# Weight blocks of a two-layer mixing kernel: when they are loaded, and in which tiles

## The chip, the core and the metric

The kernel runs on one core of one Trainium2 chip. A core has five engines that each work through their own instructions in order and wait for each other by semaphores: TensorE (PE, matmuls), VectorE (DVE), ScalarE (ACT), GpSimd (POOL), and SyncE (SP), which here only issues DMAs. The metric is the time of one execution on the device in microseconds. All times are of one program on one core.

## The reference

Everything is float32 in the reference. Its third part, in which the change lies, is this (batch 8, 576 tokens, 512 channels, 256 hidden tokens, 1536 hidden channels):

```python
def _moe2_ref(x, w_tok1, w_tok2, w_ch1, w_ch2) -> np.ndarray:
    xt = x.transpose(0, 2, 1)
    h = np.maximum(xt @ w_tok1, 0.0) @ w_tok2
    u = x + h.transpose(0, 2, 1)
    h2 = np.maximum(u @ w_ch1, 0.0) @ w_ch2
    return (u + h2).astype(np.float32)
```

Before it stand an attention over pooled keys (`_attn_ref`) and a first mixing `_moe_ref`, that ends in `u + relu(u @ w_ch)`; its result is the `x` above. The inputs arrive as float64 words (the host does no arithmetic), so a weight has to be turned into float32 on the chip before it is used.

## The kernel before

**Numbers.** A float32 value is kept as a pair of values in a rounded format, a high part and a rest (`h`, `l`), and a product is three matmuls: high by high, high by rest, rest by high. The high part is made by an ACT cast, the rest by a subtraction on DVE or POOL.

**Stages.** Up to about 555 us run the attention and most of the first mixing. From 555 to 779.4 us runs the *token stretch*, batch by batch (8 of them, one about every 28 us): `emit_ch` (L863 on) ends the first mixing, eight groups of 12 matmuls into one PSUM bank each, that DVE drains into `u` (L878); `emit_tr` transposes `u` on PE (L173), and ACT and DVE copy the transposes out as a pair (L893, L894); `emit_tok1` makes the hidden tokens (drained by ACT L912 and DVE L913); `emit_tok2` makes the second token product (drained by DVE L928). Then `channel_mix` does the two channel products as one level of Strassen's scheme, seven products in place of eight. The first product (779.4 to 1064.9 us) has six chunks of columns with six passes each; a pass, `first_pair(c, i)`, is 7 products of 6 matmuls of 128x384, 42 matmuls. Of them `p1` (ACT L1264), `u2` (DVE L1268), `p5` (ACT L1277, DVE L1278 and L1281) and four outputs `g` are drained. The bank of `p1` is added to again by the third product (A12), the bank of the copy at L1277 by the sixth (S4), that of L1281 by the seventh (A22), so PE can't go on with these three before ACT or DVE has read them. The second product follows (to 1335.3 us).

**Weight blocks.** `weight_steps(m, wd, tags, gaps)` (L955) writes the weights of the two channel products, in the form in which the products use them, to the DRAM tensor `scr_w[m]`: m = 0 is `w_ch1` (6 blocks of width 256), prepared during the token stretch; m = 1 is `w_ch2` (12 blocks of width 128), prepared during the first product. A block goes through these steps:

- `load`: two DMAs of the raw words into `ws`. For m = 0 each is held back by a copy of one element on ACT (L976) from the `u` drained last (`gate`).
- `conv` for two halves: ACT takes Abs (L992), DVE four operations (L993, L994, L998, L1002) that put the bits of the float32 together in `wm`.
- `sums`: POOL L1011 and L1012, DVE L1013 and L1014, that form Strassen's sums in `wsum`.
- `split` for two halves, two pieces each: ACT casts into a piece `wo` (L1023), POOL or DVE subtracts (L1024), a DMA stores the piece to `scr_w` (L1025).

The steps stand in a list `wq`, with empty steps (`gaps`) between them. `wstep()` takes one: in the token stretch after every second group of `emit_ch` and twice in `emit_tok2` (six a batch, as many as a block has), in the first product after every product.

**Order.** The program is written as a list of operations; a scheduler turns it into one order for each engine, with the place in the program as priority, and sets waits where regions of tiles overlap. Each named place in SBUF (`kr`, `vr`, `R1`, `n0` ...) holds one tile at a time. `Units` (L1072) hands out operand containers: `HOME_E` 14 for even, `HOME_O` 11 for odd chunks (`R1` 3, `e` 3, `Z0` 5). An operand takes two, a chunk's seven take 14, so the next chunk's are prepared as far as containers are free. `HOME_R` are four buffers (`n0` to `n3`) for raw columns (`raw_n`) from which operands are split (ACT L1125, DVE L1126) and differences formed (DVE L1129). At the last chunk `more_raws` makes raw buffers of the odd containers that have come free. `free_s` (from `HOME_S`) is the list of buffers that `first_pair` drains into; its outputs `g` leave by a DMA (L1258).

Of the kernel before, what the change touches and what calls it, by code (L numbers as in the profile page):

```python
# [10 lines left out]
F32R = mybir.dt.float32r  # L11
U32 = mybir.dt.uint32
# [52 lines left out]
def tile_attn_moe(  # L65
# [56 lines left out]
    def st(tag, shape, dt, name=None):  # L122
        need(tag)
        return sb.tile(shape, dt, tag=tag, name=name or tag)
# [227 lines left out]
    bdk = st("bdk", [128, 4, 144], F32)  # L352
    vbh = st("vbh", [128, 4, 128], F32R)
    vlh = st("vlh", [128, 4, 2, 64], F32R)
# [588 lines left out]
    def rotate(tags):  # L943
        n = [0]

        def alloc(shape, dt, name):
            tag = tags[n[0] % len(tags)]
            n[0] += 1
            return st(tag, shape, dt, name)

        return alloc
# [3 lines left out]
    def weight_steps(m, wd, tags, gaps):  # L955

        NH_ = 256 // wd
        quads = [(g, j, h) for g in range(3) for h in range(NH_) for j in range(2)]  # L960
        ws_t, wm_t, wsum_t, wo_t = (rotate(x) for x in tags)
        whole = wd == 128
        raw = {}

        def load(i):
            g, j, h = quads[i]
            behind = gate[0]
            if whole:
                t = ws_t([128, 2, 2, wd, 2], U32, f"ws{m}_{i}")
                t = [t[:, kk] for kk in range(2)]  # L970
            else:
                t = [ws_t([128, 2, wd, 2], U32, f"ws{m}_{i}_{kk}") for kk in range(2)]
            if behind is not None:

                for x in t:
                    nc.scalar.copy(out=x[0:1, 0, 0:1, 0].bitcast(F32), in_=behind)  # L976
            for kk in range(2):
                if m == 0:
                    src, r, c0 = w_ch1, (2 * kk + j) * 128, g * 256 + h * wd
                else:  # L980
                    src, r, c0 = w_ch2, (6 * kk + 2 * g + j) * 128, h * wd
                src = src[r:r + 128, :].bitcast(U32).rearrange("p (h c t) -> p h c t", h=2, t=2)
                nc.sync.dma_start(out=t[kk], in_=src[:, :, c0:c0 + wd, :])
            raw[i] = [t, None, None]

        def conv(i, kk):
            if kk == 0:
                raw[i][1] = wm_t([128, 2, 2, wd], F32, f"wm{m}_{i}")
            t = raw[i][0][kk]
            x = raw[i][1][:, kk]  # L990
            xu = x.bitcast(U32)
            nc.scalar.activation(out=x, in_=t[:, :, :, 1].bitcast(F32), func=ACTF.Abs)  # L992
            nc.vector.tensor_scalar(out=x, in0=x, scalar1=F64_FLOOR, scalar2=None, op0=ALU.max)  # L993
            nc.vector.tensor_scalar(  # L994
                out=xu, in0=xu, scalar1=3, scalar2=0x3FFFFFFF,
                op0=ALU.logical_shift_left, op1=ALU.bitwise_and,
            )
            nc.vector.scalar_tensor_tensor(  # L998
                out=xu, in0=t[:, :, :, 1], scalar=0xC0000000, in1=xu,
                op0=ALU.bitwise_and, op1=ALU.bitwise_or,  # L1000
            )
            nc.vector.scalar_tensor_tensor(  # L1002
                out=xu, in0=t[:, :, :, 0], scalar=29, in1=xu,
                op0=ALU.logical_shift_right, op1=ALU.bitwise_or,
            )

        def sums(i):
            x = raw[i][1]
            s = raw[i][2] = wsum_t([128, 4, wd], F32, f"wsum{m}_{i}")
            a11, a21, a12, a22 = x[:, 0, 0], x[:, 0, 1], x[:, 1, 0], x[:, 1, 1]  # L1010
            nc.gpsimd.tensor_tensor(out=s[:, 0], in0=a21, in1=a22, op=ALU.add)  # L1011
            nc.gpsimd.tensor_tensor(out=s[:, 2], in0=a11, in1=a21, op=ALU.subtract)  # L1012
            nc.vector.tensor_sub(out=s[:, 1], in0=s[:, 0], in1=a11)  # L1013
            nc.vector.tensor_sub(out=s[:, 3], in0=a12, in1=s[:, 1])  # L1014

        def split(i, half):
            x, s = raw[i][1:3]
            parts = ((x[:, 1], 2, A12, nc.gpsimd), (x[:, 0, 0:1], 1, A11, nc.gpsimd)) if half == 0 else (
                (s[:, 0:2], 2, S1, nc.vector), (s[:, 2:4], 2, S3, nc.vector))
            g, j, h = quads[i]  # L1020
            for n, (src, k, o0, eng) in enumerate(parts):
                o = wo_t([128, 2, 2, wd], F32R, f"wo{m}_{i}_{half}{n}")[:, 0:k]
                nc.scalar.copy(out=o[:, :, 0], in_=src)  # L1023
                eng.tensor_sub(out=o[:, :, 1], in0=src, in1=o[:, :, 0].bitcast(F32))  # L1024
                nc.sync.dma_start(out=scr_w[m][:, g, o0:o0 + k, j, h * 2 * wd:(h + 1) * 2 * wd],  # L1025
                                  in_=o.bitcast(F32).rearrange("p k a c -> p k (a c)"))

        def nothing():
            pass

        steps = []
        for i in range(len(quads)):
            ahead = []
            if i == 0:
                steps += [lambda: load(0)] + [nothing] * gaps[0]
            if i + 1 < len(quads):
                ahead = [lambda i=i: load(i + 1)] + [nothing] * gaps[0]
            for f, n in ((lambda i=i: conv(i, 0), gaps[1]), (lambda i=i: conv(i, 1), gaps[2])):
                steps += [f] + [nothing] * n
            if m == 1:  # L1040
                steps += ahead
            for f, n in ((lambda i=i: sums(i), gaps[3]), (lambda i=i: split(i, 0), gaps[4]),
                         (lambda i=i: split(i, 1), gaps[5])):
                steps += [f] + [nothing] * n
            if m == 0:
                steps += ahead
        return steps

    wq = []
    gate = [None]  # L1050

    def wstep(n=1):
        while wq and n > 0:
            wq.pop(0)()
            n -= 1
# [2 lines left out]

    HOME_W = [f"w{i}" for i in range(13)] + ["zt1", "q0", "q1", "pt0", "pt1", "zt0", "tmp0", "tmp1"]
    HOME_E = (("Z1", 5), ("Xh", 3), ("Xl", 3), ("R0", 3))  # L1060
    HOME_O = (("R1", 3), ("e", 3), ("Z0", 5))
    HOME_R = (("n0", 1), ("n1", 1), ("n2", 1), ("n3", 1))
    HOME_S = ["vbh", "vlh", "vbl", "vll", "bdk", "vlr", "t1", "stg1"]

    def channel_mix():
        class Units:
# [31 lines left out]
        even = Units(HOME_E, F32R, "ope")  # L1098
        odd = Units(HOME_O, F32R, "opo")
        raws = Units(HOME_R, F32, "raw")  # L1100
        free_w = list(HOME_W)
        free_s = list(HOME_S)

# [76 lines left out]
        def pump(n):  # L1180
            while queue and n > 0:
                (r, p), what, key = queue[0]
                if r > len(raws.list) or p > sum(len(u.list) for u in homes_of(key)):
                    return
                queue.pop(0)
                what()
                n -= 1

        def load_x(c):
            def go(x, blk):  # L1190
                k, t = int(blk[0]) - 1, int(blk[1]) - 1
                t0 = (2 * c + t) * NH
                nc.sync.dma_start(out=x.t, in_=scr_x[:, 2 * k:2 * k + 2, t0:t0 + NH])

            return go
# [8 lines left out]
        for c in range(NCH):  # L1204
            loads, steps = moving(load_x(c), (0, c))
# [19 lines left out]


        gate[0] = None
        wq[:] = weight_steps(1, 128, (["kr"], ["n4"], ["pl"], ["vr", "stg0"]), (2, 2, 2, 2, 3, 0))
        pump(16)
        for g in range(3):  # L1230
            for o in PO:
# [64 lines left out]
        def more_raws():  # L1296

            if any(q[2][0] == 0 for q in queue):
                return
            for tag, n in HOME_O:  # L1300
                mine = [x for x in odd.list if x[0] == tag]
# [6 lines left out]
            for i in range(6):  # L1308
                first_pair(c, i)
        wstep(1000)  # L1310
        free_s += ["stg0", "pl"]


        def load_o(c, d, k, t):
# [186 lines left out]
    if True:  # L1501
        prologue()
        for b in range(B):
            last = b == B - 1
            side = []
            f = "l_" if last else "f_" if b == 0 else ""
# [30 lines left out]
        flush()  # L1537
        cq_step(20)
        wq[:] = weight_steps(0, 256, (W_TAGS[0:4], W_TAGS[4:6], W_TAGS[6:8], W_TAGS[8:13]), (0,) * 6)
        wstep(2)  # L1540

# [37 lines left out]
        wstep(1000)  # L1579
        flush()  # L1580
        channel_mix()


# [58 lines left out]
```

## Time and profile before

| | |
|---|---|
| median of 3 runs | 1333.22 us (1333.06 to 1338.38) |
| the profiled execution's own time | 1337.11 us |
| its span, first to last instruction | 1335.3 us, mean granted PE clock 0.993 |
| PE, DVE, ACT, POOL busy | 1277.9, 976.6, 637.1, 315.5 us (96, 73, 48, 24%) |
| the chain that ended last, by engine | PE 55%, DVE 21%, issue 11%, DMA 8% |
| token stretch, 555 to 779.4 us | PE 217.01 of 224.40 us, DVE 150.67 |
| first product, 779.44 to 1064.94 us | PE 271.92 of 285.50 us, DVE 195.62 |
| end of it and second product, 1066.1 to 1335.3 us | PE 264.40 of 269.20 us |

PE is busy nearly all the time, and its matmuls are pipelined: a matmul is shown from its start to its modelled end, which overlaps the next, so a short idle time of PE is hidden in the busy figure. What a stage loses is therefore read from PE's waits, and from the time per matmul against a stretch without waits. Line numbers are those of the kernel before.

### The profile page before, as it was taken

What the parts mean: (1) busy time and instruction counts of PE and PEld (TensorE: products, weight loads), DVE (VectorE), ACT (ScalarE), POOL (GpSimd) and SP (SyncE); (2) the same over time, 40 slices, a digit from 0 to 9 for tenths busy, and PEclk for the clock granted to TensorE, in tenths of its full rate; (3) what the DMA queues carried; (4) which work ended last, traced back from release to release, by engine and by line L of the source; (5) the groups of instructions that cost most, each with busy time, mean ns of one, the idle gap of its engine ahead of it and who ended that gap; (6) DMA issues with size and microseconds to landing.
All of it is one profiled execution on the core that took longest, in us unless ns stands there. A gap on an engine that the chain in (4) does not pass through costs nothing.

```text
span 1335.3 us, 22342 instructions
## 1 busy us (share of the span) xinstructions
PE 1277.9 (96%) x8214; PEld 1216.5 (91%) x8216; DVE 976.6 (73%) x1749; ACT 637.1 (48%) x1190; POOL 315.5 (24%) x340
## 2 busy tenths in 40 slices
PE   6899999999999999999999999999999999999998
PEld 4588999999999998998889988888999999999998
DVE  7987667584958696566676768688665489987893
ACT  4765454555564564233333246466454354444442
POOL 4553324232433533111110001111100013133112
PEclk9999999999999999999999999999999999999999
DMA  9423122221322023445567367767544986556521
GB/s 330 145 81 118 58 97 81 85 91 60 108 64 69 28 89 115 145 162 211 196 237 261 128 206 256 237 202 244 202 155 166 335 318 216 163 187 208 185 94 69
DMA packets 119613, 213.70 MB, mean 160 GB/s; under 512 B 11152, under 2 KB 65936, under 8 KB 119504
## 3 DMA queue, kind: packets, MB, share of 16 engines
q1 hardware_dynamic: 119504, 212.29, 46.9%
q8 instruction: 64, 1.05, 0.3%
q14 instruction: 45, 0.37, 0.1%
HBM read 133.60 MB, written 78.64 MB: 159 GB/s over the span
## 4 chain that ended last, share of the span: by engine, by line
PE 55%; DVE 21%; issue 11%; DMA 8%; POOL 2%; ACT 2%; SPq 0%; DVEq 0%; POOLq 0%; ACTq 0%
PE x L159 20%; PE m L159 18%; PE t L159 15%; DMA scr_g<-g 2%; DVE sm L564 2%; PE x L173 2%; DVE e L553 2%; DVE mx L552 2%; DMA raw_n<-scr_x 1%; DVE tmp L736 1%; DMA scr_w<-wo 1%; DVE sm L565 1%; POOL wo L1024 1%; DMA ws<-w_ch 1%; DVE R L789 1%
## 5 line engine op out<-in xcount | busy, mean ns | idle before, releaser
L159 PE MATMUL m<-wtk,Z 128*128 128x256 f32 (+1 forms) x1536 | 247.1, 300 | 7.4 <-DVE R L789 7.1
L159 PEld LDWEIGHTS m<-wtk,Z 128*128 128x128 f32 x1536 | 218.0, 190 | 10.7 <-DVE R L789 7.7
L751 POOL TENSOR_TENSOR Z<-tmp,Z 128x1024 fp32r<-128x1024 f32 x31 | 74.7, 2411 | 110.9 <-ACT Z L750 110.9
L1012 POOL TENSOR_TENSOR wsum<-wm 128x128 f32<-128x128 f32 (+1 forms) x18 | 10.8, 602 | 298.8 <-DVE wm L1002 281.7
L159 PE MATMUL t<-wth,Xh 128*128 128x256 f32 (+1 forms) x504 | 76.5, 293 | 0.5 <-DVE Xh L536 0.2
L1364 POOL TENSOR_TENSOR o<-o,u 128x384 f32<-128x384 f32 x12 | 16.2, 1374 | 244.5 <-DVE u L1352 156.3
L159 PEld LDWEIGHTS t<-wth,Xh 128*128 128x128 f32 x504 | 67.0, 188 | 4.5 <-DVE Xh L536 1.8
L718 DVE SCALAR_TENSOR_TENSOR tmp<-tmp,t 128x512 f32<-128x512 f32 x40 | 27.3, 684 | 53.9 <-ACT tmp L705 53.9
L159 PE MATMUL x<-ope_Xl,wa 128*128 128x384 f32 x336 | 65.4, 336 | 0.1
L159 PE MATMUL m<-ope_Z,wa 128*128 128x384 f32 x300 | 63.7, 337 | 1.3 <-ACT p L1264 0.6
L159 PE MATMUL x<-ope_R,wa 128*128 128x384 f32 x312 | 62.4, 340 | 0.7 <-DVE p L1281 0.7
L736 DVE TENSOR_TENSOR tmp<-x,tmp 128x1024 f32<-128x1024 f32 x32 | 39.1, 1221 | 31.1 <-ACT tmp L712 16.0
L159 PE MATMUL x<-ope_Z,wa 128*128 128x384 f32 x276 | 56.1, 339 | 4.4 <-ACT p L1277 2.5
L159 PEld LDWEIGHTS x<-ope_Xl,wa 128*128 128x128 f32 x336 | 58.8, 188 | 0.4 <-DVE ope_Xl L1126 0.4
L159 PE MATMUL x<-bdk,q 128*128 128x144 f32 x320 | 47.9, 303 | 11.5 <-DVE bdk L1423 7.0
L159 PEld LDWEIGHTS x<-ope_R,wa 128*128 128x128 f32 x312 | 54.6, 188 | 2.6 <-DVE p L1281 1.8
L159 PEld LDWEIGHTS x<-bdk,q 128*128 128x128 f32 x320 | 44.4, 203 | 13.6 <-issue 10.8
L159 PE MATMUL m<-wtk,zt 128*128 128x256 f32 (+1 forms) x192 | 56.8, 296 | 0.0
L159 PE MATMUL x<-ope_Xh,wa 128*128 128x384 f32 x264 | 54.9, 340 | 1.9 <-DVE p L1281 0.8
L159 PEld LDWEIGHTS m<-ope_Z,wa 128*128 128x128 f32 x300 | 52.9, 188 | 2.2 <-ACT p L1264 0.9
L159 PEld LDWEIGHTS x<-ope_Z,wa 128*128 128x128 f32 x276 | 48.2, 188 | 6.7 <-ACT p L1277 3.5
L705 ACT ACTIVATE tmp<-t,magic 128x512 f32<-128x512 f32 x40 | 27.3, 684 | 55.6 <-PE t L159 42.8
(412 smaller groups left out, 3521.6 us busy)
## 6 DMA issues: line engine op xcount, KB each, us to landing
wa<-scr_w SPq DMA_DIRECT2D x42, 512.0 KB, 5.5
scr_g<-g SPq DMA_DIRECT2D x108, 192.0 KB, 2.4
scr_w<-wo SPq DMA_DIRECT2D x42, 256.0 KB, 2.7
scr_u<-R SPq DMA_DIRECT2D x32, 288.0 KB, 2.1
u<-scr_u SPq DMA_DIRECT2D x32, 288.0 KB, 4.1
scr_w<-wo SPq DMA_DIRECT2D x18, 512.0 KB, 3.1
scr_x<-u SPq DMA_DIRECT2D x32, 288.0 KB, 2.8
raw_n<-scr_x SPq DMA_DIRECT2D x24, 384.0 KB, 3.9
```

Source lines behind the costliest of these rows:

```text
L159: nc.tensor.matmul(out=o, lhsT=l, rhs=r, start=start, stop=stop, skip_group_check=skip)
L173: nc.tensor.transpose(o, i, ident)
L552: nc.vector.tensor_reduce(out=mx[:, c0:c1, :], in_=v, axis=AX.X, op=ALU.max)
L553: nc.vector.tensor_tensor(out=e[:, c0:c1, 2 * p:2 * p + 2, :], in0=v, in1=mx[:, c0:c1, :].unsqueeze(3).to_broadcast([128, n, 2, 72]), op=A ...
L564: nc.vector.tensor_reduce(out=sm, in_=ep, axis=AX.X, op=ALU.add)
L565: nc.vector.tensor_scalar(out=sm, in0=sm, scalar1=1e-9, scalar2=8.0, op0=ALU.add, op1=ALU.mult)
L705: nc.scalar.activation(out=t, in_=pt, func=ACTF.Identity, bias=magic[:, 0:1])
L718: nc.vector.scalar_tensor_tensor(out=t, in0=t, scalar=MAGIC, in1=pt, op0=ALU.subtract, op1=ALU.subtract)
L736: nc.vector.tensor_tensor(out=tmp, in0=px.unsqueeze(1).to_broadcast([128, 2, 512]), in1=tmp, op=ALU.mult)
L751: later(1.0 if lo is nc.vector else 0.0, lambda: lo.tensor_sub(out=zl, in0=zv, in1=zh.bitcast(F32)), tg, zg)
L789: nc.vector.tensor_add(out=R[:, j, ts], in0=o, in1=R[:, j, ts])
L1364: nc.gpsimd.tensor_tensor(out=u22[d].t, in0=u22[d].t, in1=u2[d].t, op=ALU.add)
```

## The change

There are two parts. The instructions are the same on every engine, in kind and in number (PE 8012, DVE 1751, ACT 1192, POOL 345, SP 699 with repeats); what differs is where they stand, and which tiles they use.

- For m = 0 the load of the next block moves from the end of a block's steps (after the second `split`) to before its `sums`, where m = 1 has it already.
- For m = 1 `ws` becomes one tile with two halves used in turn, in `R1` (before: one tile in `kr`, a single buffer). `wo` becomes four pieces, in `kr` and `vr`, each used by the same piece of every block (before: two tiles in turn, in `vr` and `stg0`, for the four pieces). `stg0` becomes one more buffer for draining, from the start. `R1` is no container for operands any more: 22 containers in place of 25. After the first product its three thirds become raw buffers.

```diff
         whole = wd == 128
+        own = {}
         raw = {}
...
             if whole:
-                t = ws_t([128, 2, 2, wd, 2], U32, f"ws{m}_{i}")
-                t = [t[:, kk] for kk in range(2)]
+                if i == 0:
+                    own["ws"] = ws_t([128, 2, 2, 2, wd, 2], U32, f"ws{m}")
+                    own["wo"] = [x[:, k] for t in range(2) for x in [wo_t([128, 2, 2, 2, wd], F32R, f"wo{m}_{t}")]
+                                 for k in range(2)]
+                t = [own["ws"][:, i % 2, kk] for kk in range(2)]
...
-                o = wo_t([128, 2, 2, wd], F32R, f"wo{m}_{i}_{half}{n}")[:, 0:k]
+                if whole:
+                    o = own["wo"][2 * half + n][:, 0:k]
+                else:
+                    o = wo_t([128, 2, 2, wd], F32R, f"wo{m}_{i}_{half}{n}")[:, 0:k]
...
-            if m == 1:
-                steps += ahead
+            steps += ahead
             for f, n in ((lambda i=i: sums(i), gaps[3]), (lambda i=i: split(i, 0), gaps[4]),
                          (lambda i=i: split(i, 1), gaps[5])):
                 steps += [f] + [nothing] * n
-            if m == 0:
-                steps += ahead
...
-    HOME_O = (("R1", 3), ("e", 3), ("Z0", 5))
+    HOME_O = (("e", 3), ("Z0", 5))
...
-    HOME_S = ["vbh", "vlh", "vbl", "vll", "bdk", "vlr", "t1", "stg1"]
+    HOME_S = ["vbh", "vlh", "vbl", "vll", "bdk", "vlr", "t1", "stg1", "stg0"]
...
-        wq[:] = weight_steps(1, 128, (["kr"], ["n4"], ["pl"], ["vr", "stg0"]), (2, 2, 2, 2, 3, 0))
+        wq[:] = weight_steps(1, 128, (["R1"], ["n4"], ["pl"], ["kr", "vr"]), (2, 2, 2, 2, 3, 0))
...
-        free_s += ["stg0", "pl"]
+        free_s += ["pl"]
+        raws.homes["R1"] = 3
+        raws.list += [("R1", i) for i in range(3)]
```

The lines after `weight_steps` move by 4 to 7: L992 becomes L996, L993 to L1002 become L997 to L1006, L1013 and L1014 become L1017 and L1018, L1023 and L1024 become L1030 and L1031, L1125 becomes L1129, and the lines of `first_pair` move by 4 (L1264 becomes L1268, L1277 L1281, L1281 L1285).

**DVE in the token stretch.** The eight drains of a batch's `emit_ch` (`u` L878) and block 2 of `w_ch1` (`wm_2`, `wsum_2`). Before:

```order
L878 SCALAR_TENSOR_TENSOR u_6175<-x_6591,u_6175 128x256
L1002 SCALAR_TENSOR_TENSOR wm_2_6571<-ws_2_0_6537,wm_2_6571 128x512
L993 TENSOR_SCALAR wm_2_6571<-wm_2_6571 128x512
L878 SCALAR_TENSOR_TENSOR u_6175<-x_6610,u_6175 128x320
L994 TENSOR_SCALAR wm_2_6571<-wm_2_6571 128x512
L998 SCALAR_TENSOR_TENSOR wm_2_6571<-ws_2_1_6538,wm_2_6571 128x512
L878 SCALAR_TENSOR_TENSOR u_6175<-m_6624,u_6175 128x256
L1002 SCALAR_TENSOR_TENSOR wm_2_6571<-ws_2_1_6538,wm_2_6571 128x512
L1013 TENSOR_TENSOR wsum_2_6638<-wsum_2_6638,wm_2_6571 128x256
L878 SCALAR_TENSOR_TENSOR u_6175<-t_6643,u_6175 128x320
L1014 TENSOR_TENSOR wsum_2_6638<-wm_2_6571,wsum_2_6638 128x256
```

After, the rows up to the same batch's drains (`h1b` is the drain of `emit_tok1` ahead of them):

```order
L1017 TENSOR_TENSOR wsum_2_6667<-wsum_2_6667,wm_2_6571 128x256
L1018 TENSOR_TENSOR wsum_2_6667<-wm_2_6571,wsum_2_6667 128x256
L1031 TENSOR_TENSOR wo_2_10_6842<-wsum_2_6667,wo_2_10_6842 128x2x256
L913 SCALAR_TENSOR_TENSOR h1b<-t_6504,h1b 128x512
L878 SCALAR_TENSOR_TENSOR u_6173<-x_6521,u_6173 128x256
L1031 TENSOR_TENSOR wo_2_11_6846<-wsum_2_6667,wo_2_11_6846 128x2x256
L878 SCALAR_TENSOR_TENSOR u_6173<-x_6543,u_6173 128x320
L878 SCALAR_TENSOR_TENSOR u_6173<-m_6557,u_6173 128x256
L878 SCALAR_TENSOR_TENSOR u_6173<-t_6577,u_6173 128x320
L878 SCALAR_TENSOR_TENSOR u_6173<-x_6591,u_6173 128x256
L878 SCALAR_TENSOR_TENSOR u_6173<-x_6610,u_6173 128x320
L878 SCALAR_TENSOR_TENSOR u_6173<-m_6624,u_6173 128x256
```

The conversion, the sums and the pieces of block 2 stood among and behind the eight drains of `u`; all but one subtraction of a piece now stand ahead of the second drain.

**ACT in the token stretch.** The gate copies of block 3 (L976, after L980), its Abs (L992, after L996) and what stands next to them: the casts of the second half (L1023) and the copies of the transposes (`x` L893). Before:

```order
L976 COPY ws_3_0_6844<-u_6482 1x1
L976 COPY ws_3_1_6845<-u_6482 1x1
L992 ACTIVATE wm_3_6878<-ws_3_0_6844 128x512
L992 ACTIVATE wm_3_6878<-ws_3_1_6845 128x512
L1023 CAST wo_3_01_6977<-wm_3_6878 128x256
L1023 CAST wo_3_00_6973<-wm_3_6878 128x2x256
L864 CAST Xh<-u_6789 128x576 x2
L536 COPY u_6482<-u_6482 128x4x64
L1023 CAST wo_3_10_7058<-wsum_3_6945 128x2x256
L1023 CAST wo_3_11_7062<-wsum_3_6945 128x2x256
```

After:

```order
L980 COPY ws_3_0_6638<-u_6173 1x1
L980 COPY ws_3_1_6639<-u_6173 1x1
L864 CAST Xh<-u_6480 128x576 x2
L536 COPY u_6173<-u_6173 128x4x64
L864 CAST Xh<-u_6480 128x576 x2
L996 ACTIVATE wm_3_6878<-ws_3_0_6638 128x512
L893 CAST x_6693<-t_6695 128x512
L893 CAST x_6693<-x_6702 128x512
L893 CAST x_6693<-x_6709 128x512
L893 CAST x_6693<-m_6716 128x512
L896 CAST x2t<-t_6723 128x512
L996 ACTIVATE wm_3_6878<-ws_3_1_6639 128x512
```

The first Abs of the block, which waits for its load, stood among the groups of `emit_ch`, well ahead of the copies of the transposes; it now stands right ahead of them, and the second right behind.

**ACT in the first product.** Block 4 of `w_ch2` and the drains of the passes beside it. Before:

```order
L992 ACTIVATE wm_4_9281<-ws_4_9151 128x256
L1293 ACTIVATE g_9098<-g_9098 128x384
L1264 COPY p_9109<-m_9102 128x384
L992 ACTIVATE wm_4_9281<-ws_4_9151 128x256
L1023 CAST wo_3_10_9264<-wsum_3_9184 128x2x128
L1272 ACTIVATE g_9131<-m_9102 128x384
L1277 COPY p_9141<-x_9134 128x384
L1023 CAST wo_3_11_9268<-wsum_3_9184 128x2x128
L1282 ACTIVATE p_9141<-p_9141 128x384
L1023 CAST wo_4_00_9424<-wm_4_9281 128x2x128
L1287 ACTIVATE g_9163<-g_9163 128x384
L1293 ACTIVATE g_9173<-g_9173 128x384
```

After:

```order
L996 ACTIVATE wm_4_9260<-ws_8423 128x256
L1276 ACTIVATE g_8772<-m_8743 128x384
L996 ACTIVATE wm_4_9260<-ws_8423 128x256
L1281 COPY p_8782<-x_8775 128x384
L1030 CAST wo_0_8424<-wm_4_9260 128x128
L1286 ACTIVATE p_8782<-p_8782 128x384
L1291 ACTIVATE g_8807<-g_8807 128x384
L1030 CAST wo_0_8424<-wm_4_9260 128x2x128
L1297 ACTIVATE g_8817<-g_8817 128x384
L1129 CAST ope_Z_8345<-raw_n_8341 128x768
L1268 COPY p_8830<-m_8821 128x384
L1129 CAST ope_Z_8345<-raw_n_8337 128x768
```

The block's casts into pieces (L1023, after L1030) followed its conversion by about one pass, with casts of block 3 between; all steps of block 4 now stand in one pass, and the pieces of a half are parts of one tile. In the order of the changed kernel the twelve blocks stand in passes up to the 15th (counted from one `u2` to the next), in the order of the kernel before up to the 22nd.

## Rows read from the trace of the kernel before

**Rows 1.** The windows of three stages and a stretch without waits; first line: columns.

```profile
core 0: us, PE busy (x) PEld busy (x) DVE busy (x) ACT busy (x) POOL busy (x), PEclk, DMA share, GB/s
555.00:779.40 224.40, 217.01 (x1464) 204.08 (x1463) 150.67 (x278) 71.57 (x138) 18.81 (x20) 0.99 0.56 197
779.44:1064.94 285.50, 271.92 (x1514) 261.05 (x1513) 195.62 (x383) 154.40 (x325) 27.43 (x48) 1.00 0.66 221
1066.10:1100.00 33.90, 32.53 (x179) 30.57 (x178) 29.37 (x33) 17.33 (x24) 5.42 (x4) 1.00 0.89 318
1150.00:1200.00 50.00, 50.00 (x288) 50.00 (x287) 44.14 (x53) 20.30 (x28) 10.25 (x8) 1.00 0.53 170
```

**Rows 2.** What TensorE (PE) waited for, 555 to 779: us in total, times, longest.

```profile
PE x L173 <- DVE u L878: 4.0, 2, 2.2
PE t L173 <- DVE u L878: 2.2, 1, 2.2
PE x L159 <- DVE x L894: 0.5, 2, 0.3
```

**Rows 3.** The timeline of VectorE (DVE): start, duration, ..., idle before it.

```profile
612.65 1.47 DVE L1013 TENSOR_TENSOR wsum<-wsum,wm 128x256 f32<-128x256 f32 x1 [0.84 <-POOL wsum L1011]
614.04 0.48 DVE L878 SCALAR_TENSOR_TENSOR u<-t,u 128x320 f32<-128x320 f32 x1
```

**Rows 4.** The timeline of ScalarE (ACT) in the same batch.

```profile
604.99 0.67 ACT L992 ACTIVATE wm<-ws 128x512 f32<-128x512 f32 x1 [6.64 <-DMA ws<-w_ch]
```

**Rows 5.** The windows of the four microseconds that follow, as in Rows 1.

```profile
614.00:616.00 2.00, 1.42 (x7) 1.42 (x8) 2.00 (x6) 1.44 (x4) 0.00 (x0) 0.67 0.62 237
616.00:618.00 2.00, 2.00 (x10) 2.00 (x9) 2.00 (x5) 2.00 (x6) 0.00 (x0) 0.50 0.45 172
```

**Rows 6.** What PE waited for in the first product.

```profile
PE x L159 <- ACT p L1277: 5.2, 5, 2.1
PE x L159 <- DVE p L1281: 4.4, 8, 1.0
PE m L159 <- ACT p L1264: 3.8, 6, 0.9
```

**Rows 7.** What ACT waited for in the first product.

```profile
ACT wo L1023 <- DMA scr_w<-wo: 13.3, 17, 1.9
...
ACT wm L992 <- DMA ws<-w_ch: 4.7, 8, 1.5
```

**Rows 8.** The timeline of ACT around one long wait of PE.

```profile
866.84 0.30 ACT L1023 CAST wo<-wm 128x128 fp32r<-128x128 f32 x1 [1.93 <-DMA scr_w<-wo]
...
868.09 0.46 ACT L1277 COPY p<-x 128x384 f32<-128x384 f32 x1
```

**Rows 9.** The windows of 22 passes, first u2 to 23rd, and two single ones.

```profile
781.82:962.44 180.62, 167.96 (x926) 159.34 (x925) 141.33 (x296) 105.68 (x230) 27.43 (x48) 1.00 0.69 228
923.56:931.17 7.61, 7.18 (x42) 6.78 (x40) 7.18 (x13) 6.23 (x14) 0.00 (x0) 1.00 0.83 263
992.64:1000.00 7.36, 7.36 (x44) 7.26 (x43) 2.79 (x6) 2.92 (x6) 0.00 (x0) 1.00 0.30 109
```

**Rows 10.** The window of tile wm alone, first product: DVE, ACT, POOL busy.

```profile
779.44:1064.94 285.50, 44.42 (x120) 18.79 (x48) 27.43 (x48) 1.00 0.66 221
```

**Rows 11.** The window of tile wo alone, same columns.

```profile
779.44:1064.94 285.50, 9.98 (x24) 17.90 (x48) 14.81 (x24) 1.00 0.66 221
```

**Rows 12.** Groups of DVE, 785 to 965: busy us, mean ns, idle before.

```profile
L1129 DVE TENSOR_TENSOR raw_n<-raw_n,raw_n 128x768 f32<-128x768 f32 x16 | 15.3, 955 | 0.0
...
L1013 DVE TENSOR_TENSOR wsum<-wsum,wm 128x128 f32<-128x128 f32 x12 | 6.6, 546 | 5.6 <-POOL wsum L1011 5.6
L1014 DVE TENSOR_TENSOR wsum<-wm,wsum 128x128 f32<-128x128 f32 x12 | 4.4, 370 | 0.2
```

**Rows 13.** What DVE waited for in the first product.

```profile
DVE wm L993 <- ACT wm L992: 8.5, 6, 4.3
DVE wsum L1013 <- POOL wsum L1011: 5.6, 12, 0.8
```

## Prediction

> **What bounds the kernel now.** I read the windows first, then the waits of PE, then the timelines at the waits. By the windows PE is the bound throughout: 217.01 of 224.40 us in the token stretch, 271.92 of 285.50 in the first product [rows 1]. In the stretch without waits 288 matmuls of 128x384 take 50.00 us, 0.1736 each [rows 1], so the 1512 of the first product need 262.5 us; they take 285.50. The stage loses 23.0 us, and that is what a change to the work beside PE can win or add to. The quiet pass shows the same from near by: 42 matmuls by 0.1736 are 7.29 us, and it takes 7.36 [rows 9].
>
> In the token stretch the long waits are those of the transposes for drains of `emit_ch`: 4.0 us in two and 2.2 in one, then small ones behind the copies of the transposes [rows 2]. The timeline shows how they come about: the sum L1013 starts at 612.65 after 0.84 us of waiting for POOL and takes 1.47 us, and the drain of `u` that the transposes need stands behind it and starts at 614.04 [rows 3]. The block is that late because ACT waited 6.64 us for its load [rows 4]. And the pause costs more than itself: in the four microseconds after it the granted clock is 0.67, then 0.50 [rows 5], the lower of the two levels (1.2 of 2.4 GHz), which is (0.33 + 0.50) x 2 = 1.7 us of work.
>
> In the first product PE waits for three drains: 5.2 us for the copy L1277, 4.4 for L1281, 3.8 for L1264, 13.4 us in 19 waits [rows 6]. ACT itself waits 13.3 us in 17 places for stores of pieces to end before it may cast into the same tile, and 4.7 us in 8 places for loads [rows 7]. One place shows the link: the cast at 866.84 waited 1.93 us for a store, and the copy L1277, for which PE waits, stands behind it and starts at 868.09 [rows 8].
>
> **The change, part by part.** My sum goes against the profiled execution, 1337.11 us; that one lies 3.9 us above the median of 1333.22, so I take 3.9 off at the end.
>
> *Load a block ahead, token stretch.* No instruction is added. The load gets nearly a batch (28 us) where 6.64 us were missing, so Abs and the conversion move into the time of `emit_tok1`, and the sums with them; only one subtraction of a piece is left among the drains of `u`. The removable sum is: waits 4.0 + 2.2 + 0.5 = 6.7 us [rows 2], and the clock 1.7, counted at one place only, since the mean of the stretch is 0.99 [rows 1]: 8.4 us. The refill of PE's pipeline after five waits comes on top, and something new will be late: DVE does a block's work beside `emit_tok1`, and the two Abs now stand around the copies L893. I let these two cancel and take 8, between 3 (a wait of about a microsecond in each of five batches) and 11 (clock lost at all three pauses).
>
> *Four pieces and two halves of `ws`, first product.* The 13.3 + 4.7 us of ACT's waits go, since a piece's store then has a whole block's time, and the load too. They are not PE's: of PE's waits I put those down to them that have such a wait of ACT right ahead in the drains' engine, nine places, the largest the one shown [rows 8], about 7.4 of the 13.4 us, by which the stage would lose 15.6. The other 6 us, and most of the refills, are waits for DVE's and POOL's backlog, and these the change tightens: the same twelve blocks stand in passes up to the 15th, no longer to the 22nd.
>
> What this asks of DVE, from rows: a block is (44.42 + 9.98) / 12 = 4.53 us [rows 10, 11], the drains of a pass 2.79 [rows 9], a raw subtraction 0.955 [rows 12]. Passes 1 to 15 hold twelve blocks and, counted in the new order, 25 raw subtractions: 15 x 2.79 + 12 x 4.53 + 25 x 0.955 = 120.1 us, 8.0 a pass. Records overlap where one follows at once: in the whole stage 36 x 2.79 + 54.4 + 59 x 0.955 = 211 stand in 195.62 [rows 1], 0.93; so 7.0 to 7.4 us of DVE to 7.3 of PE. DVE has no room in these passes, and it also waits: 5.6 us in twelve for POOL [rows 13], 0.5 a block, while the 8.5 for Abs [rows 13] mostly go with the loads. The nearest row is a pass that was packed like that before, by raw subtractions: 7.61 us long with 7.18 of DVE [rows 9], DVE's work plus 0.4. With POOL's wait on top a dense pass takes 7.2 + 0.4 + 0.5 = 8.1. Against 36 quiet passes, 265.0 us, the stage of before loses 20.5; 22 passes in 180.62 us [rows 9] lose 180.62 - 22 x 7.36 = 18.7 of it, the others 1.8. Now fifteen at 8.1 lose 11.1, the seven that become free of blocks some 2 (an estimate, 0.25 each as in the pass of 7.61), the others 1.8 as before: 14.9 against 20.5. I take a gain of 5, from -6 (dense passes of 8.9) to +11 (7.7).
>
> Here the Trainium skill speaks against the change. The subtraction L1013, which starts with POOL's last instruction still at work, takes 0.546 us on the mean, L1014 of the same shape and kind 0.370 [rows 12]. "SBUF — State Buffer", section "Who interferes with whom", says that a DVE instruction with two SBUF inputs and a GpSimd one that reads SBUF exclude each other for a whole instruction. The rows agree in kind, at 0.18 us a block; by the page it could be all POOL does for a block, and the dense pass would be that of the first rival.
>
> *R1 no longer holds operands, `stg0` drains from the start.* Beside a chunk's 14, 8 containers are left in place of 11 for the next chunk's 14, so three more are split only when the last pass of the chunk frees its own. PE needs them in the order A11, S2, A12, S1, S3, S4, A22, the last about six products of 1.04 us later. I count nothing; a microsecond at each of five chunks is the worst, and lies in the range above.
>
> *R1 as raw buffers at the end.* From 1066.1 to 1100 PE is busy 32.53 of 33.90 us [rows 1]; three more raw buffers bring loads of the second product forward. I take 1, between 0 and 2.
>
> Sum: 8 + 5 + 1 = 14 us; 1337.1 - 14 = 1323.1, and 1319 at the median's level.
>
> **The rivals.** (a) *DVE becomes the bound, slower.* Place: passes 2 to 15. Price: POOL's 27.43 us, 2.29 a block [rows 10], stands in DVE's way: 7.2 + 2.3 + 0.4 = 9.9 us a pass, DVE and POOL never at once. Fifteen lose 38.1, with 3.8 for the rest 41.9 against 20.5: 21.4 more; less 8 and 1 it ends 12.4 later, at 1346. It decides from a dense pass of 7.36 + (20.5 + 9 - 3.8) / 15 = 9.07 on; by over 0.5% from 9.5. Against it: before, 0.18 us a block is all that the two show. (b) *Only the token stretch wins.* Packing returns what the pieces free: 1333.2 - 9 = 1324. For it: DVE's 7.0 to 7.4 of 7.3 us. (c) *The gated load is late again, in the new place.* The first Abs stands ahead of the copies L893. The gate opens after the seventh group, some 4.2 us before L893 is wanted (12 matmuls of 320 columns, 18 of 256 and 320 in `emit_tok2`, at 0.145 and 0.116 us by columns from the 0.1736 of 384, and a transposed block, 0.2); were the load as late as 6.64 us [rows 4], ACT would hold L893 for 2.4 us in the four batches of blocks 2 to 5, 10 us, and the stretch loses 2: 1333.2 + 2 - 6 = 1329. Against it: loads of `u` share the queue at the old gate, not at the new. (d) *The change doesn't do what it says*: if the two halves of `ws`, or the pieces, were still taken as one tile by the waits, the loads and casts would wait as before and only the order would change: -3 to +3, 1333.
>
> **How the numbers follow.** Forecast (all three terms) 0.50, (b) 0.22, (c) 0.10, (d) 0.05, (a) 0.13, of which half ends above 1340. A measurement of this kernel can tell about 0.5%, 6.7 us, from no change: 1326.6 and 1339.9 are the bounds. The forecast's own range is 8 to 20 us of gain, 1313 to 1325; (b) reaches from 1321 to 1328, (c) from 1325 to 1332. The range of 8 in 10 is 1308 to 1331: below it lie dense passes at 7.5 with all clock losses gone, above it (a) and (d). Faster: 0.48 of the forecast, 0.17 of (b), 0.03 of (c), 0.02 of the others, 0.70. Slower 0.07. Same 0.23.
>
> **What would show it.** Right: no wait of a transpose for `u` L878, and ACT not waiting for `ws`, from 570 to 760; the granted clock at 1.0 there; no wait of L1030 for stores; the last block's conversion at about 15 passes, near 900 us; passes 2 to 15 at 8.1 us, the quiet ones at 7.36; a first product of about 280 us. Wrong: passes with a block above 9.07 us, with L1017 or L1018 lengthened beside POOL (a); ACT waiting for a load ahead of L893 (c); L1030 still waiting for stores (d); or new waits of PE in `emit_tok1` for DVE's drains, which would leave the token stretch above 219 us.

## The result and the profile after

The changed kernel takes 1321.21 us (median of 4 runs, 1320.95 to 1325.21) against 1333.14 for the kernel before (4 runs, 1332.73 to 1338.38), a ratio of 0.9906 with a 95% interval of 0.9888 to 0.9925: by that ratio 12.5 us less, between 10.0 and 14.9. Forecast were 1319 and a gain of 14. The profiled execution has a span of 1318.9 us and is at the median; that of before was 4.0 us above its own.

The windows of the changed kernel, for the token stretch (from the first transposition of its second batch), the first product and the first 200 matmuls of the second (columns as in [rows 1]):

```profile
553.73:771.01 217.28, 215.48 (x1478) 204.02 (x1476) 154.41 (x286) 74.64 (x142) 19.31 (x21) 1.00 0.58 208
771.01:1051.81 280.80, 270.98 (x1514) 261.03 (x1513) 196.49 (x384) 152.28 (x323) 27.79 (x48) 1.00 0.68 231
1051.81:1087.10 35.29, 35.06 (x201) 34.71 (x201) 30.34 (x35) 18.80 (x26) 8.21 (x6) 1.00 0.85 301
```

The same stretches took 227.28 (552.16 to 779.44), 285.50 [rows 1] and 37.93 us (1064.94 to 1102.87) before. That is 10.0, 4.7 and 2.6 us.

What PE waited for in the changed kernel, 555 to 768 us, answers to [rows 2]:

```profile
PE t L173 <- DVE u L878: 0.9, 1, 0.9
PE m L159 <- ACT h1b L912: 0.4, 1, 0.4
PE x L173 <- DVE u L878: 0.4, 1, 0.4
```

Of 6.2 us of waits of the transposes [rows 2] 1.3 are left, and no pause of 2 us. The window 600 to 620 has a granted clock of 1.00; before it had 0.91, with the fall to 0.50 behind the pause [rows 5]. The timeline of DVE in the batch that [rows 3] shows:

```profile
598.11 1.50 DVE L1017 TENSOR_TENSOR wsum<-wsum,wm 128x256 f32<-128x256 f32 x1 [1.32 <-POOL wsum L1015]
...
600.90 0.68 DVE L913 SCALAR_TENSOR_TENSOR h1b<-t,h1b 128x512 fp32r<-128x512 f32 x1
...
610.13 0.49 DVE L878 SCALAR_TENSOR_TENSOR u<-t,u 128x320 f32<-128x320 f32 x1 [1.33 <-PE t L159]
```

The sum of the block takes 1.50 us, as it did, but ahead of the drain of `emit_tok1` (L913) and twelve microseconds before the last drain of `u`, which now waits for PE and not PE for it. The timeline of ACT there:

```profile
608.83 0.28 ACT L980 COPY ws<-u 1x1 f32<-1x1 f32 x2 [7.56 <-DVE u L878]
...
613.01 0.70 ACT L996 ACTIVATE wm<-ws 128x512 f32<-128x512 f32 x1 [0.71 <-DMA ws<-w_ch]
613.61 0.58 ACT L893 CAST x<-t 128x512 fp32r<-128x512 f32 x1
```

The gate is 0.28 us of copies at 608.83, the Abs of the first half starts 4.2 us later after 0.71 us of waiting for its load, and the copy L893 directly behind it.

What PE and ACT waited for in the first product (768 to 1053 us), which answers to [rows 6, 7]:

```profile
PE m L159 <- ACT p L1268: 5.0, 6, 1.6
PE x L159 <- DVE p L1285: 3.4, 5, 1.3
PE x L159 <- ACT p L1281: 1.1, 2, 0.7
```

```profile
ACT ope_Xl L1129 <- DMA raw_n<-scr_x: 2.6, 1, 2.6
...
ACT wm L996 <- DMA ws<-w_ch: 1.0, 2, 0.6
ACT wo L1030 <- DMA scr_w<-wo: 0.7, 1, 0.7
```

PE's waits fall from 13.4 us to 9.5, ACT's for stores from 13.3 to 0.7 and for loads from 4.7 to 1.0. The rest is another mix: the copy of `p1` (L1268) leads, held by casts of operands that wait for raw columns (2.6 us at one place). The fifteen passes that hold the twelve blocks, from the first `u2` to the sixteenth:

```profile
773.66:896.19 122.53, 114.36 (x630) 108.52 (x629) 108.49 (x246) 76.59 (x177) 27.79 (x48) 1.00 0.81 273
```

122.53 / 15 = 8.17 us a pass, with DVE busy 108.49 / 15 = 7.23. Counted from the stage's start in passes of 42 matmuls, the first fifteen and the next seven were, before and after:

```profile
779.44:903.64 124.20, 114.86 (x632) 108.59 (x631) 97.36 (x201) 72.25 (x155) 18.57 (x32) 1.00 0.69 226
903.64:960.07 56.43, 53.11 (x295) 50.75 (x295) 44.78 (x95) 33.70 (x75) 8.86 (x16) 1.00 0.70 237
...
771.01:893.84 122.83, 114.66 (x633) 108.82 (x632) 110.41 (x247) 76.42 (x177) 27.79 (x48) 1.00 0.81 272
893.84:946.76 52.92, 52.09 (x295) 50.77 (x295) 28.96 (x47) 25.70 (x50) 0.00 (x0) 1.00 0.43 151
```

All of POOL's 48 instructions for the blocks, in place of 32, now stand in the first fifteen passes, which take nearly as long as before. The gain stands behind them, in seven passes that are free of blocks. The groups of DVE from 768 to 900 us, which answer to [rows 12]:

```profile
L1017 DVE TENSOR_TENSOR wsum<-wsum,wm 128x128 f32<-128x128 f32 x12 | 8.0, 663 | 4.0 <-POOL wsum L1015 3.8
L998 DVE TENSOR_SCALAR wm<-wm 128x256 uint32<-128x256 uint32 x24 | 7.2, 314 | 0.1
...
L1018 DVE TENSOR_TENSOR wsum<-wm,wsum 128x128 f32<-128x128 f32 x12 | 4.5, 377 | 0.2
```

The sum L1017 has grown from 546 to 663 ns on the mean.

### The profile page after: what moved, and what is told of

Read it like the earlier page. It is cut to its first block, busy times and chain, and to the rows that moved or that the text cites. A ratio compares the mean times of both kernels' runs of the same rounds, so it can differ in the third digit from the quotient of the medians.

```text
span 1318.9 us, 22347 instructions
## 1 busy us (share of the span) xinstructions
PE 1271.3 (96%) x8214; PEld 1214.2 (92%) x8216; DVE 978.1 (74%) x1749; ACT 635.8 (48%) x1190; POOL 318.6 (24%) x340
## 5 line engine op out<-in xcount | busy, mean ns | idle before, releaser
L159 PE MATMUL x<-ope_Z,wa 128*128 128x384 f32 x492 | 94.8, 336 | 0.9 <-ACT p L1281 0.7
L159 PEld LDWEIGHTS x<-ope_Z,wa 128*128 128x128 f32 x492 | 86.2, 188 | 1.5 <-ACT p L1281 1.5
L159 PE MATMUL x<-ope_R,wa 128*128 128x384 f32 x324 | 69.7, 339 | 1.6 <-DVE p L1285 1.6
L159 PE MATMUL x<-ope_Xl,wa 128*128 128x384 f32 x288 | 60.1, 336 | 0.0
L159 PE MATMUL t<-ope_Z,wa 128*128 128x384 f32 x276 | 56.8, 336 | 0.0
L569 POOL TENSOR_TENSOR e<-e,sm 128x720 f32<-128x720 f32 x32 | 45.1, 1408 | 30.6 <-DVE sm L568 30.0
L159 PEld LDWEIGHTS x<-ope_Xl,wa 128*128 128x128 f32 x288 | 50.8, 188 | 0.0
L558 ACT ACTIVATE e<-e 128x720 f32<-128x720 f32 x32 | 25.7, 804 | 50.7 <-DVE e L553 50.6
```

What stands on the lines that cost most here:

```text
L159: nc.tensor.matmul(out=o, lhsT=l, rhs=r, start=start, stop=stop, skip_group_check=skip)
L558: nc.scalar.activation(out=ep, in_=ep, func=ACTF.Exp, scale=1.0 / 64.0)
L569: nc.gpsimd.tensor_tensor(out=ep, in0=ep, in1=sm.unsqueeze(3).to_broadcast([128, 5, 2, 72]), op=ALU.mult)
```

## The experiments

Stage lengths are from one profile each: the token stretch from the first transposition (L173) after 500 us to the first matmul of the first product, the first product from there to the first matmul of the second, the second from there to the end of the last matmul. Times are medians, ratios go against the kernel before beside it (0.9906 for the changed kernel). What lies before the token stretch differs by up to 5 us between executions of the same instructions (517.6 to 522.5 us), so small differences are read from the stages. Single passes are counted in PE's 42 matmuls, in the first product. A profile shows one execution, not always one at the median: that of before lies 4.0 us above the median in the result, e6's 4.1 above and e11's 3.1 below their own; and the same order does not give the same stage twice, as e5 shows.

| kernel | token | first | second | us | ratio (95%) |
|---|---|---|---|---|---|
| before, profiled twice | 259.69, 258.81 | 285.50, 283.70 | 266.92, 267.84 | 1333.14 | 1 |
| changed | 249.69 | 280.80 | 263.62 | 1321.21 | 0.9906 (0.9888 to 0.9925) |
| e1 token part | 250.26 | 282.84 | 266.36 | 1323.92 | 0.9928 (0.9904 to 0.9953) |
| e2 product part | 256.84 | 281.14 | 263.62 | 1330.80 | 0.9970 (0.9952 to 0.9989) |
| e3 single ws | 249.49 | 286.69 | 263.62 | 1324.70 | 0.9920 (0.9898 to 0.9942) |
| e4 two pieces | 249.79 | 285.32 | 263.62 | 1323.83 | 0.9920 (0.9895 to 0.9945) |
| e5 raws later | 249.13 | 284.22 | 263.98 | 1322.06 | 0.9903 (0.9880 to 0.9925) |
| e6 rests on POOL | 250.71 | 293.24 | 263.61 | 1328.31 | 0.9949 (0.9931 to 0.9968) |
| e7 POOL twice | 249.68 | 288.56 | 263.62 | 1329.26 | 0.9955 (0.9940 to 0.9970) |
| e8 sums on DVE | 249.79 | 279.15 | 263.62 | 1317.81 | 0.9863 (0.9845 to 0.9881) |
| e9 all on DVE | 249.32 | 275.12 | 263.64 | 1315.20 | 0.9844 (0.9824 to 0.9863) |
| e10 R1 raws early | 249.21 | 283.43 | 263.81 | 1320.88 | 0.9881 (0.9858 to 0.9904) |
| e11 e9 and e10 | 249.57 | 272.22 | 263.84 | 1311.57 | 0.9818 (0.9795 to 0.9840) |

**e0, the kernel before again.** 

> The kernel before once more, with a new profile, since the execution profiled first (1337.11 us) lies 3.9 us above the median of its runs. Theory: the surplus lies in one or two places, and the stages lose the same elsewhere: a span of about 1331.5 us, token stretch (first transposes to first matmul of the channel product) 223 to 227 us, first product 285 +- 1. Rival: the surplus lies in the first product, which is then 281 to 282 us, and the change won nothing there.

1337.14 us, span 1334.5. The surplus did not go away, so it isn't one odd place; the kernel before scattered from 1331.3 to 1338.7 us over 17 runs. The first product took 283.70, within 2 us of the first profile and nearer to the theory than to the rival; the token stretch, counted as expected, took 226.05.

**e1 and e2, one part each.** The edit of e1, against the kernel before; e2 is the changed kernel with this edit undone:

```diff
-            if m == 1:
-                steps += ahead
+            steps += ahead
...
-            if m == 0:
-                steps += ahead
```

> Only the first part: the load of the next w_ch1 block stands before the sums; the second part is left as before. Theory (token stretch and first product each win their own): 1325 us (-8), token stretch as in the changed kernel (217 us), first product as before. Rival 1 (the token stretch makes all of the gain): 1321 to 1322. Rival 2 (its gain in the profile was an odd pause of one execution): 1329 or above.

> Only the second part: double ws, four pieces, 22 containers, R1 as raw buffers at the end; the load of w_ch1 blocks as before. Theory: 1328.5 us (-4.5), first product 281 us, the token stretch as before. Rival 1 (the packed passes give all back): 1333. Rival 2 (most of the gain is here): 1325.

e1: 0.9928, -9.6 us, with a token stretch of 250.26. e2: 0.9970, -4.0 us, with a first product of 281.14 and a second of 263.62. Both theories hold: that of e1 (its token stretch, counted as expected, is 217.49 us), and that of e2 (a gain of 4.5 was forecast). The two add up (-13.6 to the measured -12.5). In three executions with the order of before the first product took 284.0 us on the mean (285.50, 283.70, 282.84), in two with the new one 281.0: 3.0 us. But e5 below has the order of the changed kernel in this stage, on every engine, and took 284.22; with it the new mean is 282.1, the gain 2.0 us, and the two groups overlap. The times say less still: e2 gained 4.0 us (1.5 to 6.4), of which the second product's shorter stage makes 3.4. That the first product won is clear of the scatter in one place, passes 16 to 22: 56.4 to 57.2 us in the three with the old order, 52.7 to 53.1 with the new one. The first fifteen took 121.6 to 124.2 and 122.8 to 125.9, the last fourteen about 0.8 us more than before.

**e3 and e4, the halves of the second part.** The first edit is e3's, the second e4's:

```diff
-                t = [own["ws"][:, i % 2, kk] for kk in range(2)]
+                t = [own["ws"][:, 0, kk] for kk in range(2)]
...
-                    o = own["wo"][2 * half + n][:, 0:k]
+                    o = own["wo"][2 * n][:, 0:k]
```

> The changed kernel, but both uses of ws in the second part take the same half, so the next block's load waits for the end of the conversion as before. Theory (the four pieces make the gain in the first product, since 13.3 us of ACT's waits were theirs against 4.7 for loads): 1322 us, +1, first product 281.5. Rival (the loads make it): 1325, first product 284 to 285, with ACT waiting for ws.

> The changed kernel with two piece buffers used in turn in place of four (double ws stays). With a single ws the first product took 286.7 us, so the loads weigh more than I thought. Theory A (both halves of the second part are needed; ACT waits for stores again, some 10 us in about 15 places): first product 283 to 285 us, total 1324 to 1325. Theory B (double ws is the whole gain of that stage): first product 281, total 1321, though ACT waits for stores.

e3 speaks against my theory and for the rival: four pieces with a single `ws` take 286.69 us, longer than before, with ACT waiting 8.8 us for loads in 13 places. e4 gives theory A: 285.32 us, and ACT waits for stores again. The waits of ACT, of e3 and of e4:

```profile
ACT wm L996 <- DMA ws<-w_ch: 8.8, 13, 1.5
...
ACT wo L1030 <- DMA scr_w<-wo: 0.5, 1, 0.5
```

```profile
ACT wo L1030 <- DMA scr_w<-wo: 11.8, 14, 2.3
...
ACT wm L996 <- DMA ws<-w_ch: 1.3, 1, 1.3
```

One wait removed alone leaves the other. e3 loses in the packed passes (128.11 us for the first fifteen), e4 behind them (56.58 us for passes 16 to 22, in which its last blocks still stand). That only both together win is not shown clear of the scatter: by time both stand at 0.9920, within the interval of the changed kernel, and e5 took 284.22 us with nothing taken away.

**e5, R1 as raw buffers later.** The three lines stand behind the first product `prod(A11, X, True)` of `second_chunk(0)`.

> The changed kernel, but the three thirds of R1 become raw buffers only after the first product of 36 matmuls of the second stage, some 6 us later in the program. The second stage took 263.62 us in both kernels with the second part and 266.4 to 267.8 in the three without. Theory (the three raw buffers at hand bring the loads of its first operands forward): 266 to 268 us, total +3, 1324. Rival (something else of the second part, as which containers hold the operands, makes the 3 us): 263.6, total 1321.

263.98 us: the rival's time, but the experiment did not do what it was for. The first load into an R1 buffer was issued 161 us ahead of the second stage in both kernels, since the scheduler moves it up. (The first product, whose order is that of the changed kernel, has one pass of 11.82 us here: a cast of an operand, with the copy L1268 behind it, waits 2.55 us for its raw columns, where the changed kernel's waited 0.71.) What differs between the groups of kernels are the loads into `e`. SP's queue, of the kernel before and of the changed one (second stage from 1064.94 and 1051.81):

```profile
1060.62 2.06 SPq L1200 DMA_DIRECT2D raw_R<-scr_g  x2
...
1063.19 0.43 SPq L1200 DMA_DIRECT2D raw_R<-scr_g  x1
...
1068.65 0.32 SPq L1200 DMA_DIRECT2D raw_e<-scr_g  x1
...
1071.72 0.39 SPq L1200 DMA_DIRECT2D raw_e<-scr_g  x1
...
1076.21 0.32 SPq L1200 DMA_DIRECT2D raw_e<-scr_g  x1
```

```profile
1007.20 0.38 SPq L1204 DMA_DIRECT2D raw_e<-scr_g  x1
...
1009.40 0.42 SPq L1204 DMA_DIRECT2D raw_e<-scr_g  x1
...
1011.66 0.42 SPq L1204 DMA_DIRECT2D raw_e<-scr_g  x1
```

Loads into `e` stand 3.7 to 11.3 us after the start before, 40 to 45 us ahead of it now, and PE's waits for splits there are nearly gone (0.2 us in place of 1.1). The lines `raw_R` of before show that R1's three were raw buffers there too, by `more_raws`, 1.8 to 4.3 us ahead of the second product. That the smaller set of odd containers empties `e` a chunk earlier is how I read it; it was not tried alone, since the second stage can't be fed without the R1 buffers.

**e6 and e7, more on POOL.** The first edit is e6's, the second e7's:

```diff
-                (s[:, 0:2], 2, S1, nc.vector), (s[:, 2:4], 2, S3, nc.vector))
+                (s[:, 0:2], 2, S1, (nc.vector, nc.gpsimd)[m]), (s[:, 2:4], 2, S3, (nc.vector, nc.gpsimd)[m]))
...
-                eng.tensor_sub(out=o[:, :, 1], in0=src, in1=o[:, :, 0].bitcast(F32))
+                for _ in range(2 if m == 1 and half == 0 else 1):
+                    eng.tensor_sub(out=o[:, :, 1], in0=src, in1=o[:, :, 0].bitcast(F32))
```

> The changed kernel with the subtractions of the second half's pieces of w_ch2 on POOL in place of DVE (24 of them, 0.42 us on DVE, about 0.74 on POOL). Theory (DVE's own work bounds the packed passes, 8.17 us on the mean): DVE has 0.84 us less in each, so passes 1 to 15 fall to 7.7 on the mean, the stage to 275 us, the total to 1316. Rival (POOL is in DVE's way and its backlog is what PE waits for): no gain, 281 to 285 us, 1321 to 1325.

> The changed kernel with POOL's subtractions of w_ch2 (two a block, 0.62 us on the mean) done twice, with the same result. Theory (POOL lengthens only the DVE instructions with two SBUF inputs that it meets, by some 0.25 us each, and DVE's own work is the bound): 1 to 3 us, total 1322 to 1324. Rival (POOL excludes DVE for whole instructions, or its backlog bounds): up to 1.24 us a block, 10 to 15 us, total 1331 or above.

Both miss my theory: less work on DVE made the stage 12.4 us longer, past the rival's range too, and POOL's 16.1 us more (43.91 against 27.79) made it 7.8 longer, between theory and rival. By time, 0.9949 and 0.9955 against 0.9906, it is 5.7 and 6.5 us: e6's profiled execution was a long one, and has a pass of 11.24 us at the place of e5's. The timelines of POOL and DVE in e6 show what the two engines do to each other:

```profile
793.03 0.88 POOL L1031 TENSOR_TENSOR wo<-wsum,wo 128x256 fp32r<-128x256 f32 x1 [0.26 <-DVE wm L997]
...
799.54 1.50 POOL L1031 TENSOR_TENSOR wo<-wsum,wo 128x256 fp32r<-128x256 f32 x2
```

```profile
793.35 0.84 DVE L1002 SCALAR_TENSOR_TENSOR wm<-ws,wm 128x256 uint32<-128x256 uint32 x1
...
794.59 0.41 DVE L1006 SCALAR_TENSOR_TENSOR wm<-ws,wm 128x256 uint32<-128x256 uint32 x1
...
800.47 0.72 DVE L998 TENSOR_SCALAR wm<-wm 128x256 uint32<-128x256 uint32 x1
801.23 0.43 DVE L1002 SCALAR_TENSOR_TENSOR wm<-ws,wm 128x256 uint32<-128x256 uint32 x1
```

L1002 starts at 793.35, while POOL works, and ends at 794.19, 0.28 us after POOL's instruction does (793.91); L1006, of the same shape and kind, takes 0.41 with POOL idle. L998 ends at 801.19, 0.15 us behind POOL's pair (801.04), and takes 0.72 against 0.29. DVE does not go slower beside POOL, it stands until POOL is done. The first product of the changed kernel shows it as a rule: 27 DVE instructions with all inputs in SBUF begin while POOL is at work and end after it. Their own time alone is 0.29 us (128x128, and L998), 0.42 (L1002, L1006) or 0.56 (128x384); they end 0.15, 0.28 or 0.42 us behind POOL's end, however long POOL still had to go (one 0.48, which met POOL's last 0.08 us). It goes the other way too: 18 of POOL's begin beside such a DVE instruction and end 0.32 or 0.60 us behind it, with 0.46 and 0.74 alone. Each remainder is the time alone less 0.14 us. Two engines that shared a rate would not end like that.

**e8 and e9, nothing on POOL.** e8 puts the two sums on DVE, e9 the two subtractions too.

```diff
-            nc.gpsimd.tensor_tensor(out=s[:, 0], in0=a21, in1=a22, op=ALU.add)
-            nc.gpsimd.tensor_tensor(out=s[:, 2], in0=a11, in1=a21, op=ALU.subtract)
+            eng = (nc.gpsimd, nc.vector)[m]
+            eng.tensor_tensor(out=s[:, 0], in0=a21, in1=a22, op=ALU.add)
+            eng.tensor_tensor(out=s[:, 2], in0=a11, in1=a21, op=ALU.subtract)
```

> The changed kernel with POOL's two sums of a w_ch2 block (128x128) on DVE. Theory (POOL and DVE exclude each other for whole instructions, so what POOL does in a packed pass is paid by DVE too: L1017 takes 0.66 us there against 0.28 alone, after 0.32 us of waiting for POOL): DVE gets 2 x 0.28 us more a block and is spared 0.4 to 0.7, so the stage ends 0 to 3 us shorter, 278 to 281, total 1318 to 1321. Rival (only DVE's own work counts): 0.56 x 12 = 7 us more, stage 287, total 1328.

> As before it, and POOL's two subtractions a block (0.28 and 0.42 us alone on DVE) on DVE too: POOL does nothing in the first product. Theory (exclusion): DVE has 1.26 us more a block and loses all of the lengthening, some 0.7 to 0.8, and the waits, 0.3: stage 280 to 285, total 1320 to 1325, with every DVE instruction of the blocks at its short time (L1006 0.41, L1017 0.28). Rival (DVE's own work): 15 us more, stage 295, total 1336.

279.15 and 275.12 us: the rival (DVE's own work alone) is refuted, and e8 lies where the theory put it; e9 lies below even the theory's 280 to 285. e9 gives DVE 48 instructions more and takes 5.7 us off the stage, 8.3 off the time by the ratios. Its groups of DVE, to be read against those of the changed kernel above (L1018 is the sum that was L1017):

```profile
L998 DVE TENSOR_SCALAR wm<-wm 128x256 uint32<-128x256 uint32 x24 | 6.6, 288 | 0.1
...
L1018 DVE TENSOR_TENSOR wsum<-wsum,wm 128x128 f32<-128x128 f32 x12 | 3.4, 285 | 0.1
```

The sum takes 285 ns in place of 663 and waits for nobody. Exclusion alone does not add up to the gain, though: DVE is spared some 7.6 us of lengthening (by the groups' means) and 4.0 of waiting for POOL's sums, and takes over 15.3 us of work; it is busy 199.46 us in the stage, 196.49 in the changed kernel. What fell are PE's waits, from 9.5 us to 4.7, those for DVE's copy L1285 from 3.4 to 0.5. That drains held up behind POOL cost more than DVE's own time is my reading; that a block's chain is shorter without POOL's slower instructions is a rival that no run separates from it.

**e10 and e11.** e10 uses gaps (1, 1, 1, 1, 1, 0) and gives the thirds of R1 to the raw buffers once `wq` is empty; e11 is e9 with that.

> The changed kernel with gaps (1, 1, 1, 1, 1, 0), so that the list of steps is empty sooner, and the thirds of R1 given to the raw buffers then and not after the stage. Theory (the long passes at the chunks' ends, as the 25th with 8.62 us, wait for a raw load that had no buffer sooner): the passes 24 to 31 fall to 7.4, -1 to -2 us, stage 279, total 1319 to 1320. Rival (the casts of operands stand ahead of the copy L1268 in ACT's order whatever the buffers): no change, 1321.

> The kernel with POOL's work of the w_ch2 blocks on DVE (1315.2 us, stage 275.12) together with the R1 thirds as raw buffers as soon as the list of steps is empty, which took the 25th pass from 8.62 to 7.55 us. Theory (the two add up: one long pass at a chunk's end in the fourth and fifth chunk goes): stage 273 to 274.5, total 1313 to 1315. Rival (the surplus passes of the other kernel with early R1, 283.43 us as a stage, come from the shorter gaps): 276 to 278, total 1316 to 1318.

e10: the 25th pass falls from 8.62 to 7.55 us as expected, but other passes are longer (one 10.65) and the total says nothing either way. e11 has the lowest time of all, 1311.57 us, 0.9818 (0.9795 to 0.9840), stage 272.22: better than the theory, though its interval meets that of e9 and its profiled execution was the fastest of five. The 25th pass takes 7.56 us, 8.55 in e9. The shorter gaps did no harm there.

## Why the prediction was right, and where its sizes were off

- *Token stretch, 8 us taken, 8.7 measured* by stages (258.4 us on the mean of three profiles with the old order, 249.7 with the new one); e1 alone shows 9.6 by time (6.3 to 12.8). The mechanism was right at each step. Rival (c) is in the trace in small: in three batches ACT waited 0.6 to 0.7 us for a load right ahead of L893, and the longest wait, 3.3 us, stands ahead of the casts L864; PE waited for none of it.
- *First product, 5 taken, 2.0 to 3.0 measured by stages* (4.7 between the two profiles, but see e5; by time the other two terms leave it about half a microsecond). The dense pass was forecast at 8.1 us and is 8.17 (8.37 in e5); DVE's share at 7.0 to 7.4 and is 7.23; the other 21 passes lose 280.80 - 122.53 - 21 x 7.36 = 3.7 us, as forecast (3.8). The term that was mis-sized is what the kernel before lost: the 20.5 us are one execution's, whose stage is 1.5 us above the mean of three.
- *"The 13.3 + 4.7 us of ACT's waits go"*: they did, all but 1.7 us. But the 7.4 us of PE's waits that I put down to them did not go from the packed passes, which are as long as before with all twelve blocks in them; PE's waits in the stage fell by 3.9 us. In e3 I had put most on the pieces, and its profile speaks for the loads; how the two share it stays open.
- *R1 as raw buffers, 1 taken, 0 to 2 allowed: 3.4 measured* (267.0 us on the mean of three, 263.62 now). Here the step failed in its cause as well: "three more raw buffers" is not so, since R1's three became raw buffers in the kernel before too. Of R1's loads one now stands far ahead; the loads into `e` moved by about 50 us. If that comes of the 22 containers, as I read it, "I count nothing" had the wrong sign; against it stands the 0.8 us that the last fourteen passes of the first product lost.
- *Rival (a).* I gave it 0.13 and argued "0.18 us a block is all that the two show". That was a misreading: L1014, which I took as undisturbed, takes 0.29 us alone and was itself held up in two of twelve. The rival's price was wrong, its mechanism right: "SBUF — State Buffer", section "Who interferes with whom", in the Trainium skill says that the loser waits for the whole instruction, and e6's rows agree to within 0.3 us. In the order of before 19 DVE instructions ended behind POOL in this way, 27 in the changed kernel; in packed passes L1017 alone pays 0.38 us a block. Why it did not decide is a reading: POOL's 2.3 us a block overlap DVE's waits and its drains from PSUM in part. The drains L1285 and L1290 take 0.55 us in e6, and in e7, where they stand a line lower, as in the changed kernel. The same section of the Trainium skill also counts `tensor_scalar` (here with one SBUF input) among what can take the shared ports under conditions, and L998's 0.72 us agrees.
- *The clock* came back to 1.00 with the pauses gone: from 0.91 in the 20 us from 600 to 620, 1.8 us for the 1.7 counted.
- The terms' errors (+0.7, -2 to -3, +2.4) nearly cancel. The stages' sum is 14.1 to 15.1 us, at the upper end of the interval of the times (10.0 to 14.9). Two of the three profiles with the old order are of executions at 1337.1 us, so it may be too large; the 3.9 us taken off at the end were not looked for in the stages. That the total came within 2.2 us is partly luck.

## What to carry to other kernels

When a producer off the critical path is in-order and feeds two buffers, look for the second wait before removing the first: here neither alone gave a shorter stage in its profile. Look also where the gain lands: the work that was packed more tightly freed the passes behind it, and not its own. Price an engine that "has room" (POOL at 24%) by what it does to its neighbour while it runs, not by its own busy share: giving its work to the fuller engine gained more here than packing the blocks had. And a container that is taken away moves everything that would have used it; look where its successors stand before writing "nothing".

## What the runs showed of the hardware that was not expected

Work moved from GpSimd to VectorE made the stage shorter although VectorE was the fuller engine: 27.79 us of GpSimd work gone, 48 instructions of VectorE more (0.28 to 0.42 us each), and 5.7 us gained. VectorE instructions that read PSUM kept their times beside GpSimd (25 overlapped in the changed kernel's first product, none took more than 0.56 us). Of those with all inputs in SBUF the one that came second, on either engine, ended its own time alone less 0.14 us behind the other's end.
